# Seven products in place of eight: the experts' first matmuls by Strassen's scheme over 2x2 blocks, in three token passes

## The chip, the cores and the metric

The kernel runs on one core of a Trainium2 chip. The metric is the device time of one launch in microseconds (us). A core has five engines that run side by side and wait for each other by semaphores: TensorE (PE, with its weight loads shown apart as PEld), VectorE (DVE), ScalarE (ACT), GpSimd (POOL) and SyncE (SP), which here only issues the DMAs. Matmul results land in PSUM, eight banks of 512 float32 values per partition; DVE and ACT read them from there, POOL does not touch them in this kernel.

## The reference

Block-causal attention feeds a two-layer MLP with a leaky ReLU, and that feeds eight experts. Every token goes through every expert; a gate, normalised eight times over rows and columns (Sinkhorn), weighs the results.

```python
x = attention(q, k, v)                           # (2304, 512)
x = np.maximum(0.01 * h, h) @ w_out              # h = x @ w_in; (512, 2048), (2048, 512): the "GLU" stage here
logits = x @ w_gate                              # w_gate (512, 8)
P = np.exp(logits - logits.max())
for _ in range(8):
    P /= P.sum(1, keepdims=True) + 1e-09
    P /= P.sum(0, keepdims=True) + 1e-09
    P *= N / E
for e in range(8):                               # w1[e] (512, 1024), w2[e] (1024, 512)
    out += P[:, e:e + 1] * (np.maximum(x @ w1[e], 0.0) @ w2[e])
```

## The kernel before

The program has three stages. Attention comes first; it is the same in both kernels. Then comes the MLP, worked as two "experts" without a gate (e = 0 and 1, `NG` = 2), and then the eight real experts (e = 2 to 9). A float32 value is held as two float32r numbers, a high part and the rest, so a product of two values is three matmuls: high by high, high by low, low by high.

An expert is taken whole before the next. Its 2304 tokens go in five blocks (512, 512, 512, 384, 384), and the 1024 hidden columns in eight chunks of 128. `hidden(e, b, f)` (L483) multiplies one chunk of `w1` (stationary, four steps of 128 over the 512 inputs) with one block of tokens (moving): 4 x 3 = 12 matmuls into one bank of `ps_h`. ACT then takes the ReLU into the high part (L504), DVE the rest (L505). `second(e, b, f)` (L511) multiplies the hidden values (stationary, 128 tokens at a time) with 512 columns of `w2`: three matmuls for each 128 tokens (L525), summed over the eight chunks in up to four banks of `ps_o`. At the last chunk DVE multiplies each bank by its column of gate weights and adds it to the accumulator `acc` (L559). In the list `todo` the first products run two chunks ahead of the second ones.

The weights of the next expert are loaded during the last block (SP, 512 KB each), split by ACT (L118) and DVE (L119). The gate logits are float32r products of a split gate with the split tokens, 16 columns wide, turned back by float32 transposes (L566 to L586). The Sinkhorn steps follow one per chunk during the first expert; each column sum is one float32 matmul with a matrix of ones (L610).

The code gives a program order; a scheduler with a timeline model then sets the order of instructions on each engine, and each engine runs its own list strictly in order.

Of the kernel before, what the change touches and what calls it, by code (L numbers as in the profile page):

```python
# [15 lines left out]
P = 128  # L16
# [20 lines left out]
def block_attention_mlp_moe(  # L37
# [38 lines left out]
    xpool = ctx.enter_context(tc.tile_pool(name="xpool", bufs=1))  # L76
# [357 lines left out]
    n = 1  # L434
# [8 lines left out]
    with (  # L443
# [12 lines left out]
    hpool = ctx.enter_context(tc.tile_pool(name="hpool", bufs=4))  # L456
    gpool = ctx.enter_context(tc.tile_pool(name="gpool", bufs=1))
    ps_h = ctx.enter_context(tc.tile_pool(name="ps_h", bufs=4, space=bass.MemoryType.PSUM))
    ps_o = ctx.enter_context(tc.tile_pool(name="ps_o", bufs=1, space=bass.MemoryType.PSUM))

    acc = apool.tile([P, TT * DM], F32, name="acc")
    acc_x = acc.rearrange("p (c t) -> p c t", c=KC)
    acc_o = acc.rearrange("p (t d) -> p t d", d=DM)
    gate_raw = const.tile([P, KC, E], F32, name="gate_raw")
    gate = const.tile([P, KC, 2, E], F32R, name="gate")
# [6 lines left out]
    logl = const.tile([P, TT, E], F32, name="logl")  # L472

    nc.gpsimd.memset(ones, 1.0)
    nc.sync.dma_start(out=gate_raw, in_=w_gate.rearrange("(c p) e -> p c e", p=P))
    nc.gpsimd.tensor_copy(out=gate[:, :, 0, :], in_=gate_raw)
    nc.gpsimd.tensor_tensor(
        out=gate[:, :, 1, :], in0=gate_raw, in1=f32(gate[:, :, 0, :]), op=ALU.subtract
    )

    hid, o_ps = {}, {}

    def hidden(e, b, f):  # L483
# [13 lines left out]
        if e < NG:  # L497
            g = gpool.tile([P, 512], F32, name="g", tag="g")
            nc.scalar.activation(out=g[:, 0:n], in_=ps[:, 0:n], func=AF.Copy, scale=NEG_SLOPE)  # L499
            nc.vector.tensor_tensor(out=g[:, 0:n], in0=ps[:, 0:n], in1=g[:, 0:n], op=ALU.max)  # L500
            nc.scalar.copy(out=hi[:, 0:n], in_=g[:, 0:n])  # L501
            nc.vector.tensor_tensor(out=lo[:, 0:n], in0=g[:, 0:n], in1=f32(hi[:, 0:n]), op=ALU.subtract)
        else:
            nc.scalar.activation(out=hi[:, 0:n], in_=ps[:, 0:n], func=AF.Relu)  # L504
            nc.vector.scalar_tensor_tensor(  # L505
                out=lo[:, 0:n], in0=ps[:, 0:n], scalar=0.0, in1=f32(hi[:, 0:n]),
                op0=ALU.max, op1=ALU.subtract,
            )
        hid[e, b, f] = (hi, lo)

    def second(e, b, f):  # L511
        t0, n = blocks[b]
        wh, wl = (w.rearrange("p (j d) -> p j d", j=2)[:, f % 2, :] for w in w_part[2, e, f // 2])
        hi, lo = hid.pop((e, b, f))
        n_out = KC if e < NG else n // P
        for s in range(n_out):
            if f == 0:
                o_ps[s] = ps_o.tile([P, 512], F32, name=f"o{s}", tag=f"o{s}")
            cut = slice(s * P, (s + 1) * P)
            for m, (w, h) in enumerate(((wh, hi), (wl, hi), (wh, lo))):  # L520
                first, last = f == 0 and m == 0, f == FC - 1 and m == 2
                if e < NG:
                    nc.tensor.matmul(o_ps[s][:, 0:n], w[:, cut], h[:, 0:n], start=first, stop=last)  # L523
                else:
                    nc.tensor.matmul(o_ps[s], h[:, cut], w, start=first, stop=last)  # L525
            if f == FC - 1:
                evict(e, b, s)

    p_ready = [False]
    owed, later = [], []  # L530

    def evict(e, b, s):
        t0, n = blocks[b]
        if e < NG:
            a = acc_x[:, s, t0:t0 + n]
            if e == 0:
                nc.scalar.copy(out=a, in_=o_ps[s][:, 0:n])  # L537
                return
            nc.vector.tensor_tensor(out=a, in0=o_ps[s][:, 0:n], in1=a, op=ALU.add)
            if e < NG - 1:  # L540
                return

            def split():
                hi = xh[:, s, t0:t0 + n]
                nc.scalar.copy(out=hi, in_=a)
                nc.vector.tensor_tensor(out=xl[:, s, t0:t0 + n], in0=a, in1=f32(hi), op=ALU.subtract)

            later.append(split)
            return
        t = t0 // P + s  # L550
        x = e - NG
        a = acc_o[:, t, :]
        if x == 0 and not p_ready[0]:
            nc.scalar.copy(out=a, in_=o_ps[s])
            owed.append(t)
        elif x == 0:
            nc.vector.tensor_scalar(out=a, in0=o_ps[s], scalar1=pr[:, t, 0:1], scalar2=None, op0=ALU.mult)
        else:
            nc.vector.scalar_tensor_tensor(  # L559
                out=a, in0=o_ps[s], scalar=pr[:, t, x:x + 1], in1=a, op0=ALU.mult, op1=ALU.add  # L560
            )
        if x == E - 1:
            nc.sync.dma_start(out=out[t * P:(t + 1) * P, :], in_=a)


    def gate_block(b):  # L566
        t0, n = blocks[b]
        ps = ps_h.tile([P, 512], F32, name="l_ps", tag="h")
        for c in range(KC):
            for s, x in enumerate((xh, xl)):  # L570
                nc.tensor.matmul(  # L571
                    ps[0:2 * E, 0:n], gate[:, c].rearrange("p s e -> p (s e)"), x[:, c, t0:t0 + n],
                    start=c == 0 and s == 0, stop=c == KC - 1 and s == 1,
                )
        logT = gpool.tile([P, 512], F32, name="logT", tag="g")
        nc.scalar.copy(out=logT[0:2 * E, 0:n], in_=ps[0:2 * E, 0:n])
        m = n // P
        turned = ps_h.tile([P, 512], F32, name="t_ps", tag="h")
        for t in range(m):
            nc.tensor.transpose(  # L580
                turned[:, t * 2 * E:(t + 1) * 2 * E], logT[0:2 * E, t * P:(t + 1) * P], ident[0:2 * E, 0:2 * E]
            )
        both = turned[:, 0:m * 2 * E].rearrange("p (t s e) -> p t s e", s=2, e=E)
        ts = slice(t0 // P, t0 // P + m)
        nc.scalar.copy(out=logl[:, ts, :], in_=both[:, :, 1, :])
        nc.vector.tensor_tensor(out=pr[:, ts, :], in0=both[:, :, 0, :], in1=logl[:, ts, :], op=ALU.add)  # L586
# [8 lines left out]

    cs_ps = {}
# [11 lines left out]
    def sums():  # L608
        ps = ps_h.tile([P, 512], F32, name="c_ps", tag="h")
        nc.tensor.matmul(ps[:, 0:E], ones, st["cs"], start=True, stop=True)  # L610
        cs_ps[0] = ps

    def columns():
        cr = st["cr"]
        nc.vector.tensor_scalar(out=cr, in0=cs_ps[0][:, 0:E], scalar1=EPS, scalar2=None, op0=ALU.add)
        nc.vector.reciprocal(out=cr, in_=cr)
        nc.vector.tensor_tensor(
            out=pr, in0=pr, in1=cr.unsqueeze(1).to_broadcast([P, TT, E]), op=ALU.mult
        )
        nc.vector.tensor_scalar(out=pr, in0=pr, scalar1=float(NT) / E, scalar2=None, op0=ALU.mult)  # L620

    def settle():
        p_ready[0] = True
        for t in owed:
            a = acc_o[:, t, :]
# [3 lines left out]
    steps = [lambda: gate_block(NB - 1), gate_max, gate_exp]  # L629
    for _ in range(SINKHORN):  # L630
        steps += [rows, lambda: (sums(), columns())]
    steps.append(settle)


# [14 lines left out]
    for m, (e, b, f) in enumerate(todo):  # L649
# [20 lines left out]
        if later and f > 1:  # L670
            later.pop(0)()
# [35 lines left out]
```

## Time and profile before

| | us |
|---|---|
| three timed runs, median (lowest to highest) | 2255.51 (2254.02 to 2257.34) |
| the profiled execution | 2257.6 |
| its span, first to last instruction | 2255.8 |
| PE busy in the span | 2228.7 (99%) |
| PEld busy | 1898.6 (84%) |
| DVE busy | 803.9 (36%) |
| ACT busy | 549.1 (24%) |
| POOL busy | 135.1 (6%) |

The times are read against the span; the 1.8 us between span and time lie before the first and behind the last instruction. Matmuls are pipelined: one is drawn as 0.33 to 0.39 us long, but the next one starts before it ends, so the price of a matmul is the distance from its start to the start of the next. Attention and the change of float64 weights to float32 fill the first 250 us, the GLU stage goes on to about 670 us, and the experts take the rest.

### The profile page before, as it was taken

The numbers are of one execution on the slowest core, as the hardware profiler recorded it, in microseconds if no ns is written. First come the engines' busy times: TensorE is split into PE (matmuls) and PEld (weight loads), VectorE is DVE, ScalarE is ACT, GpSimd is POOL, SyncE is SP. The second block draws the span as 40 slices with busy tenths as digits, with TensorE's granted clock in tenths as the row PEclk, the third lists the DMA queues.
The fourth block names the chain that finished last, engine by engine and source line by source line (L and its number), as shares of the span: only waits on it lengthen the run. The fifth ranks groups of instructions, "written<-read, shape, count | busy, mean of one in ns | idle before, by whom it ended". The sixth has DMA issues, their size and how long they took to land.

```text
span 2255.8 us, 25881 instructions
## 1 busy us (share of the span) xinstructions
PE 2228.7 (99%) x10714; PEld 1898.6 (84%) x10714; DVE 803.9 (36%) x1514; ACT 549.1 (24%) x1145; POOL 135.1 (6%) x153
## 2 busy tenths in 40 slices
PE   7999999999999999999999999999999999999999
PEld 6777777988898898888888888888888888888888
DVE  8999666333351242123212312321231232123121
ACT  6777422332341112112111211211121121112110
POOL 3443321000000000000000000000000000000000
PEclk9999999999999999999999999999999999999999
DMA  4333143110020002002000200200020020001010
GB/s 106 87 87 73 52 125 119 38 38 1 1 75 1 1 10 66 1 1 66 10 1 10 66 1 1 66 10 1 10 66 1 1 66 10 1 10 47 19 38 28
DMA packets 106021, 79.28 MB, mean 35 GB/s; under 512 B 60592, under 2 KB 91312, under 8 KB 105904
## 3 DMA queue, kind: packets, MB, share of 16 engines
q1 hardware_dynamic: 105904, 77.63, 11.8%
q8 instruction: 84, 1.38, 0.3%
q14 instruction: 33, 0.27, 0.0%
HBM read 68.70 MB, written 8.91 MB: 34 GB/s over the span
## 4 chain that ended last, share of the span: by engine, by line
PE 84%; DVE 0%; ACT 0%; DVEq 0%; issue 0%
PE h_ps L491 42%; PE o L525 35%; PE o L523 7%; PE l_ps L571 0%; PE t_ps L580 0%; DVE acc L559 0%; PE c_ps L610 0%; DVEq L702 0%; ACT hh L501 0%; DVE g L500 0%; ACT acc L537 0%; DVE wb L153 0%
## 5 line engine op out<-in xcount | busy, mean ns | idle before, releaser
L491 PE MATMUL h_ps<-xh,w1h 128*128 128x512 f32 (+1 forms) x1600 | 590.9, 369 | 0.0
L491 PE MATMUL h_ps<-xh,w1l 128*128 128x512 f32 (+1 forms) x1600 | 589.5, 368 | 0.0
L491 PE MATMUL h_ps<-xl,w1h 128*128 128x512 f32 (+1 forms) x1600 | 589.1, 368 | 0.0
L505 DVE SCALAR_TENSOR_TENSOR hl<-h_ps,hh 128x512 fp32r<-128x512 f32 (+1 forms) x320 | 203.8, 637 | 948.0 <-ACT hh L504 947.9
L504 ACT ACTIVATE hh<-h_ps 128x512 fp32r<-128x512 f32 (+1 forms) x320 | 177.7, 555 | 1194.9 <-PE h_ps L491 1191.2
L525 PE MATMUL o<-w2l,hh 128*128 128x512 f32 x1152 | 450.4, 391 | 0.0
L525 PE MATMUL o<-w2h,hl 128*128 128x512 f32 x1152 | 449.3, 391 | 0.0
L525 PE MATMUL o<-w2h,hh 128*128 128x512 f32 x1152 | 446.9, 389 | 0.0
L491 PEld LDWEIGHTS h_ps<-xh,w1h 128*128 128x128 f32 x1600 | 301.1, 188 | 43.2
L491 PEld LDWEIGHTS h_ps<-xl,w1h 128*128 128x128 f32 x1600 | 300.8, 188 | 42.4
L491 PEld LDWEIGHTS h_ps<-xh,w1l 128*128 128x128 f32 x1600 | 300.7, 188 | 38.6
L525 PEld LDWEIGHTS o<-w2h,hl 128*128 128x128 f32 x1152 | 216.2, 188 | 45.3
L525 PEld LDWEIGHTS o<-w2l,hh 128*128 128x128 f32 x1152 | 216.3, 188 | 41.9
L525 PEld LDWEIGHTS o<-w2h,hh 128*128 128x128 f32 x1152 | 216.1, 188 | 41.2
L559 DVE SCALAR_TENSOR_TENSOR acc<-o,pr,acc 128x512 f32<-128x512 f32 x126 | 88.8, 744 | 119.4 <-PE o L525 119.4
L523 PE MATMUL o<-hh,w2h 128*128 128x512 f32 (+1 forms) x320 | 118.5, 370 | 4.6 <-ACT acc L537 4.6
L523 PE MATMUL o<-hh,w2l 128*128 128x512 f32 (+1 forms) x320 | 118.3, 370 | 0.0
L523 PE MATMUL o<-hl,w2h 128*128 128x512 f32 (+1 forms) x320 | 116.4, 370 | 0.0
L360 PE MATMUL av<-at,vz 128*128 128x448 f32 (+3 forms) x320 | 97.3, 428 | 0.0
L500 DVE TENSOR_TENSOR g<-h_ps,g 128x512 f32<-128x512 f32 (+1 forms) x80 | 50.8, 635 | 108.9 <-ACT g L499 108.7
L315 ACT ACTIVATE ex<-sc,nmax 128x288 f32<-128x288 f32 (+8 forms) x160 | 81.4, 515 | 29.7 <-DVE nmax L310 27.7
L499 ACT ACTIVATE g<-h_ps 128x512 f32<-128x512 f32 (+1 forms) x80 | 44.4, 555 | 143.1 <-PE h_ps L491 111.7
(110 smaller groups left out, 1643.3 us busy)
## 6 DMA issues: line engine op xcount, KB each, us to landing
wraw<-in_moe_w_dram SPq DMA_DIRECT2D x64, 512.0 KB, 3.6
wraw<-in_moe_w_in_dram SPq DMA_DIRECT2D x16, 512.0 KB, 3.9
wraw<-in_moe_w_out_dram SPq DMA_DIRECT2D x16, 512.0 KB, 3.7
out_dram<-acc SPq DMA_DIRECT2D x18, 256.0 KB, 2.1
qraw<-in_q_dram SPq DMA_DIRECT2D x32, 128.0 KB, 2.5
kraw<-in_k_dram SPq DMA_DIRECT2D x32, 128.0 KB, 2.5
vz<-in_v_dram SPq DMA_DIRECT2D x32, 128.0 KB, 2.4
s_in<-wa SPq DMA_DIRECT2D x8, 256.0 KB, 3.2
```

The costliest lines, as they stand in the source:

```text
L315: nc.scalar.activation(out=ex[p % 2][:, off[i] + lo:off[i] + hi], in_=part[s], func=AF.Exp, bias=nm[:, x:x + 1], scale=1.0, accum_out=sm[: ...
L360: nc.tensor.matmul(av[p][:, 512 + P * max(c - 1, 0):512 + S - P], lhsT, a[:, q0:, :], start=c == 0 and h == 0, stop=c == NKC - 1 and h == 1,)
L491: nc.tensor.matmul(ps[:, 0:n], w[:, c, cols], x, start=c == 0 and s == 0, stop=c == KC - 1 and s == 2,)
L499: nc.scalar.activation(out=g[:, 0:n], in_=ps[:, 0:n], func=AF.Copy, scale=NEG_SLOPE)
L500: nc.vector.tensor_tensor(out=g[:, 0:n], in0=ps[:, 0:n], in1=g[:, 0:n], op=ALU.max)
L504: nc.scalar.activation(out=hi[:, 0:n], in_=ps[:, 0:n], func=AF.Relu)
L505: nc.vector.scalar_tensor_tensor(out=lo[:, 0:n], in0=ps[:, 0:n], scalar=0.0, in1=f32(hi[:, 0:n]), op0=ALU.max, op1=ALU.subtract,)
L523: nc.tensor.matmul(o_ps[s][:, 0:n], w[:, cut], h[:, 0:n], start=first, stop=last)
L525: nc.tensor.matmul(o_ps[s], h[:, cut], w, start=first, stop=last)
L559: nc.vector.scalar_tensor_tensor(out=a, in0=o_ps[s], scalar=pr[:, t, x:x + 1], in1=a, op0=ALU.mult, op1=ALU.add)
```

## The change

The GLU stage stays as it was; its output now goes into three tiles `xa[0..2]` of 768 tokens (`TP`), each `[128, 4 x 768]` float32. Where a block of the GLU stage crosses a border between them, its eviction is cut in two.

The experts no longer run expert by expert over all tokens. Three passes of 768 tokens stand outside, the eight experts inside, and in each expert four groups of 256 hidden columns: 96 groups. In a group the first product is a 2x2 block product: `w1` is cut in 2 x 2 blocks (256 inputs by 128 hidden columns), the tokens in 2 x 2 blocks (256 inputs by 384 tokens). Strassen's scheme, in Winograd's form, needs seven block products for it, each two steps of 128 inputs by three matmuls, 384 columns wide, so 42 matmuls. They are named after the weight block that they use: A11, S1, A12, S2, S4, S3, A22. Three banks take them, and a bank is read while its sum is still growing: bank X takes A11 (ACT copies it out as `s1`), then S2 on top (copied as `s2`), then S3 (read for quarter 22), then A22 (quarter 21); bank Y takes S1 (copied as `s5`) and S4; bank Z takes A12. Three of the four quarters of the result add one kept copy on DVE before the ReLU (`c11`, `c12`, `c22`).

The sums of weight blocks are made by POOL, four subtractions or additions of 256 columns for each group, and then split by ACT and DVE. The sums of token blocks are made once per pass (`x_step`): four subtractions of 768 columns on POOL, seven splits of 768 columns on ACT and DVE, into the place where the split input of the GLU stage stood (`xpart` in place of `xpool`). The splits of the next pass are made in the last group of the pass before.

The second products stay 512 wide with three matmuls for each 128 tokens and 128 hidden columns. They are now `combine(n, t)`: twelve matmuls for one tile of 128 tokens, over the two groups of a pair, three tiles in each group and two to three groups behind the first products. Each tile is then added to the output once per pair of groups.

The weights of an expert are loaded and split once per pass, so three times. The gate is a native float32 product: the tokens are stationary, the eight gate columns moving, 72 matmuls of 8 columns (`gate_part`), with no transposes.

```diff
-    todo = [(e, b, f) for e in range(NE) for b in range(NB) for f in range(FC)]
+    todo = [(e, b, f) for e in range(NG) for b in range(NB) for f in range(FC)]
...
+    def gate_part(p, t0, n, ps):
+        for t in range(t0, t0 + n):
+            for c in range(KC):
+                nc.tensor.matmul(
+                    ps[:, t * E:(t + 1) * E], xv[p][:, c, t * P:(t + 1) * P], gate[:, c, :],
+                    start=c == 0, stop=c == KC - 1,
+                )
...
+    groups = [(p, e, i) for p in range(NPASS) for e in range(E) for i in range(NI)]
+    terms = ("A11", "S1", "A12", "S2", "S4", "S3", "A22")
...
+            nc.gpsimd.tensor_tensor(out=one[:, 0], in0=a21, in1=a22, op=ALU.add)
+            nc.gpsimd.tensor_tensor(out=one[:, 1], in0=one[:, 0], in1=a11, op=ALU.subtract)
+            nc.gpsimd.tensor_tensor(out=two[:, 0], in0=a11, in1=a21, op=ALU.subtract)
+            nc.gpsimd.tensor_tensor(out=two[:, 1], in0=a12, in1=one[:, 1], op=ALU.subtract)
...
+        return [
+            sums,
+            part("A", 0, 2, lambda: t["raw"][:, :, 0:P]),
+            part("A", 2, 3, lambda: t["raw"][:, 2:4, P:2 * P]),
+            part("S", 0, 2, lambda: t["one"]),
+            part("S", 2, 4, lambda: t["two"]),
+        ]
...
+        if change:
+            nc.gpsimd.tensor_tensor(out=src, in0=change[0], in1=change[1], op=ALU.subtract)
+        hi, lo = (xpart.tile([P, 2, HT], F32R, name=f"x{n}{k}", tag=f"x{n}{k}") for n in "hl")
+        nc.scalar.copy(out=hi, in_=src)
+        nc.vector.tensor_tensor(out=lo, in0=src, in1=f32(hi), op=ALU.subtract)
...
+    def product(n, k, name, first):
+        if first:
+            bank[n, name] = ps_h.tile([P, 512], F32, name="h_ps", tag="h")
+        ps = bank[n, name][:, 0:HT]
+        (wh, wl), (bh, bl) = wq.pop((n, k)), bq[groups[n][0], k]
+        for c in range(2):
+            for s, (w, x) in enumerate(((wh, bh), (wh, bl), (wl, bh))):
+                nc.tensor.matmul(
+                    ps, w[:, c], x[:, c], start=first and c == 0 and s == 0, stop=c == 1 and s == 2,
+                    skip_group_check=True,
+                )
+    def keep(n, name, k):
+        t = part[n, k] = mpool.tile([P, HT], F32, name=k, tag=k)
+        nc.scalar.copy(out=t, in_=bank[n, name][:, 0:HT])
+    def quarter(n, k, name, add):
+        x = bank[n, name][:, 0:HT]
+        if add:
+            c = mpool.tile([P, HT], F32, name=f"c{k}", tag=f"c{k}")
+            nc.vector.tensor_tensor(out=c, in0=x, in1=part[n, add], op=ALU.add)
+            x = c
...
+        nc.scalar.activation(out=hi, in_=x, func=AF.Relu)
+        nc.vector.scalar_tensor_tensor(out=lo, in0=x, scalar=0.0, in1=f32(hi), op0=ALU.max, op1=ALU.subtract)
...
+        product(n, "A11", "X", True)
+        keep(n, "X", "s1")
...
+        units[0]()
+        if n:
+            tail(n - 1)
...
+        units[1]()
...
+        product(n, "S1", "Y", True)
+        keep(n, "Y", "s5")
+        product(n, "S2", "X", False)
+        keep(n, "X", "s2")
...
+        units[2]()
...
+        product(n, "A12", "Z", True)
+        quarter(n, "11", "Z", "s1")
+        product(n, "S4", "Y", False)
+        quarter(n, "12", "Y", "s2")
+        product(n, "S3", "X", False)
+        quarter(n, "22", "X", "s5")
```

How the change moves the order on the engines, at three places. A number behind a name only tells one buffer of that name from another.

First, PE in the middle of the experts. Before, twelve first products (`h_ps`, 384 or 512 wide) and the second products of one chunk (`o0` to `o3`) take turns; these rows are such a border:

```order
L491 MATMUL h_ps_11727<-xh_70,w1h_10863 128x384
L491 MATMUL h_ps_11727<-xl_71,w1h_10863 128x384
L491 MATMUL h_ps_11727<-xh_70,w1l_10864 128x384
L525 MATMUL o0_11537<-w2h_11069,hh_11682 128x512
L525 MATMUL o0_11537<-w2l_11070,hh_11682 128x512
L525 MATMUL o0_11537<-w2h_11069,hl_11683 128x512
```

In the changed kernel this is the start of an even group of pass 1. Behind S3 of the group before (here left out) and A11 stand two half-done tiles, `o1` and `o2`, which read the older group (`h12_11743`, `h22_11754`); these rows are their end and what follows:

```order
L708 MATMUL o2_11942<-w2l_11630,h22_11754 128x512
L708 MATMUL o2_11942<-w2h_11629,h22_11754 128x512
L672 MATMUL h_ps_11958<-xhS1_10427,w1h_11801 128x384
L672 MATMUL h_ps_11958<-xlS1_10428,w1h_11801 128x384
L672 MATMUL h_ps_11958<-xhS1_10427,w1l_11802 128x384
L672 MATMUL h_ps_11958<-xhS1_10427,w1h_11801 128x384
L708 MATMUL o1_11909<-w2h_11766,h12_11880 128x512
L708 MATMUL o1_11909<-w2l_11767,h12_11880 128x512
L708 MATMUL o2_11942<-w2h_11766,h12_11880 128x512
L672 MATMUL h_ps_11757<-xhA22_10553,w1h_11666 128x384
L672 MATMUL h_ps_11757<-xlA22_10554,w1h_11666 128x384
L708 MATMUL o1_11909<-w2h_11766,h12_11880 128x512
```

The quarters of the group just finished (`h12_11880`, and later `h22_11891`) are read only after A11, twelve second products and most of S1, and A22 of the group before is pushed in between.

Second, DVE at the same place. Before, there is one instruction per chunk (`hl`) and now and then an eviction into `acc`:

```order
L505 SCALAR_TENSOR_TENSOR hl_10276<-h_ps_10262,hh_10275 128x512
L559 SCALAR_TENSOR_TENSOR acc_2962<-o0_10101,pr_2965,acc_2962 128x512
L505 SCALAR_TENSOR_TENSOR hl_10305<-h_ps_10291,hh_10304 128x512
L559 SCALAR_TENSOR_TENSOR acc_2962<-o1_10105,pr_2965,acc_2962 128x512
L559 SCALAR_TENSOR_TENSOR acc_2962<-o2_10109,pr_2965,acc_2962 128x512
L559 SCALAR_TENSOR_TENSOR acc_2962<-o3_10113,pr_2965,acc_2962 128x512
```

After, the three additions and the lower parts of the quarters stand among the splits of the weights of later groups:

```order
L685 TENSOR_TENSOR c11_11867<-h_ps_11860,s1_11764 128x384
L685 TENSOR_TENSOR c12_11878<-h_ps_11821,s2_11836 128x384
L691 SCALAR_TENSOR_TENSOR h11_11869<-c11_11867,h11_11869 128x384
L685 TENSOR_TENSOR c22_11889<-h_ps_11757,s5_11828 128x384
L691 SCALAR_TENSOR_TENSOR h12_11880<-c12_11878,h12_11880 128x384
L640 TENSOR_TENSOR w1l_11941<-wraw_11858,w1h_11940 128x512
L640 TENSOR_TENSOR w1l_11941<-wraw_11858,w1h_11940 128x256
L119 TENSOR_TENSOR w2l_12041<-wraw_11907,w2h_12040 128x1024
L691 SCALAR_TENSOR_TENSOR h22_11891<-c22_11889,h22_11891 128x384
```

Three weight splits have come between `h12` and `h22`, both of which the second products above read.

Third, DVE where the GLU stage ends. Before, the evictions of the last block (`acc<-o`) and the split of its four parts (`xl`) stand among the first experts' work:

```order
L505 SCALAR_TENSOR_TENSOR hl_6042<-h_ps_6028,hh_6041 128x512
L539 TENSOR_TENSOR acc_2962<-o0_5818,acc_2962 128x384
L505 SCALAR_TENSOR_TENSOR hl_6079<-h_ps_6065,hh_6078 128x512
L539 TENSOR_TENSOR acc_2962<-o1_5822,acc_2962 128x384
L539 TENSOR_TENSOR acc_2962<-o2_5826,acc_2962 128x384
L546 TENSOR_TENSOR xl_71<-acc_2962,xh_70 128x384
```

After, the token blocks of pass 0 (`xl` and a term's name) are split there, 768 columns at a time, and the last GLU chunk's `hl` stands among them:

```order
L500 TENSOR_TENSOR g_5979<-h_ps_5964,g_5979 128x384
L660 TENSOR_TENSOR xlA11_6040<-xa0_2962,xhA11_6039 128x768
L660 TENSOR_TENSOR xlA12_6049<-xa0_2962,xhA12_6048 128x768
L660 TENSOR_TENSOR xlS4_6058<-xa0_2962,xhS4_6057 128x768
L119 TENSOR_TENSOR w2l_6303<-wraw_6196,w2h_6302 128x1024
L502 TENSOR_TENSOR hl_5978<-g_5979,hh_5977 128x384
L660 TENSOR_TENSOR xlS1_6045<-xa0_2962,xhS1_6044 128x768
L660 TENSOR_TENSOR xlS3_6063<-xa0_2962,xhS3_6062 128x768
L525 TENSOR_TENSOR xa2_2964<-o0_5796,xa2_2964 128x384
L525 TENSOR_TENSOR xa2_2964<-o1_5800,xa2_2964 128x384
```

Seven splits of 768 columns have moved into a stretch that had splits of 384.

## Rows read from the trace of the kernel before

**Rows 1.** Busy time in the experts' stretch: engine busy (instructions), clock, DMA share, GB/s.
```profile
700.00:2230.00 1530.00, 1530.00 (x7075) 1307.30 (x7074) 371.70 (x581) 235.74 (x380) 0.38 (x1) 1.00 0.07 22
```

**Rows 2.** Longest wait of the run: engine line <- releaser: us, times, longest.
```profile
ACT hh L504 <- PE h_ps L491: 1191.2, 291, 5.1
```

**Rows 3.** Timeline of PE, 512 wide, 48 matmuls apart: start, length, instruction.
```profile
960.63 0.39 PE L491 MATMUL h_ps<-xh,w1h 128*128 128x512 f32 x1
...
971.51 0.39 PE L491 MATMUL h_ps<-xh,w1h 128*128 128x512 f32 x1
```

**Rows 4.** Timeline of PE, 384 wide, 37 matmuls apart.
```profile
443.79 0.33 PE L491 MATMUL h_ps<-xh,w1h 128*128 128x384 f32 x1
...
450.20 0.33 PE L523 MATMUL o<-hh,w2l 128*128 128x384 f32 x1
```

**Rows 5.** Busy time over one whole expert, columns as in rows 1.
```profile
960.79:1158.32 197.53, 197.53 (x913) 168.83 (x913) 46.73 (x68) 30.23 (x48) 0.00 (x0) 1.00 0.07 22
```

**Rows 6.** Timeline of PE around a float32 matmul, 8 columns wide.
```profile
733.75 0.39 PE L525 MATMUL o<-w2h,hl 128*128 128x512 f32 x1
...
733.97 0.28 PE L610 MATMUL c_ps<-cs,ones 128*128 128x8 f32 x2
...
734.43 0.39 PE L491 MATMUL h_ps<-xl,w1h 128*128 128x512 f32 x1
```

**Rows 7.** Timeline of PE around the gate's transposes.
```profile
705.58 0.39 PE L525 MATMUL o<-w2h,hh 128*128 128x512 f32 x1
...
705.90 0.35 PE L580 MATMUL t_ps<-ident,logT 16*128 16x16 f32 x3
...
706.52 0.39 PE L491 MATMUL h_ps<-xl,w1h 128*128 128x512 f32 x1
```

**Rows 8.** Groups by shape, experts: count | busy us, mean ns | idle before.
```profile
L559 DVE SCALAR_TENSOR_TENSOR acc<-o,pr,acc 128x512 f32<-128x512 f32 x123 | 86.8, 744 | 114.7 <-PE o L525 114.7
L505 DVE SCALAR_TENSOR_TENSOR hl<-h_ps,hh 128x384 fp32r<-128x384 f32 x124 | 68.9, 556 | 258.1 <-ACT hh L504 258.0
L504 ACT ACTIVATE hh<-h_ps 128x384 fp32r<-128x384 f32 x124 | 60.8, 491 | 325.2 <-PE h_ps L491 321.5 <-DVE hl L505 3.7
L119 DVE TENSOR_TENSOR w1l<-wraw,w1h 128x1024 fp32r<-128x1024 f32 x28 | 34.3, 1223 | 78.8 <-ACT w1h L118 78.8
L602 DVE RECIPROCAL rs<-rs 128x18 f32<-128x18 f32 x8 | 2.1, 267 | 0.3
```

**Rows 9.** Groups by shape, GLU stage from 440 us on, columns as in rows 8.
```profile
L546 DVE TENSOR_TENSOR xl<-acc,xh 128x512 fp32r<-128x512 f32 x12 | 7.8, 685 | 0.1
L545 ACT CAST xh<-acc 128x512 fp32r<-128x512 f32 x12 | 7.4, 622 | 3.3 <-DVE acc L539 3.2
```

**Rows 10.** Timeline of POOL and DVE in the GLU stage.
```profile
258.05 0.26 POOL L477 TENSOR_TENSOR gate<-gate_raw,gate 128x32 fp32r<-128x32 f32 x1
...
260.94 1.30 POOL L190 TENSOR_TENSOR wa<-wa,w2h 128x512 f32<-128x512 f32 x1 [2.64 <-ACT g L499]
261.46 1.33 DVE L171 SCALAR_TENSOR_TENSOR wb<-wraw,wb 128x512 f32<-128x512 uint32 x1
...
334.95 0.68 DVE L171 SCALAR_TENSOR_TENSOR wb<-wraw,wb 128x512 f32<-128x512 uint32 x1
```

**Rows 11.** DMA issues: out<-in, count, size, median us to landing.
```profile
wraw<-in_moe_w_dram SPq DMA_DIRECT2D x64, 512.0 KB, 3.6
```

**Rows 12.** Busy time (DVE, ACT) of instructions on the gate tile in the Sinkhorn stretch.
```profile
706.60:827.50 120.90, 13.05 (x42) 0.42 (x1) 1.00 0.00 1
```

**Rows 13.** Line 590 on POOL: duration ns min/median/max, first and last start.
```profile
L590 POOLq MODIFY_POOL_CONFIG  x2: 11/11/11, 383.7 to 383.8; - x2
L590 POOL PARTITION_ALL_REDUCE gall<-gmax x1: 382/382/382, 707.2 to 707.2; - x1
```

**Rows 14.** Timeline of the end of the run.
```profile
2250.16 0.84 PE L525 MATMUL o<-w2h,hl 128*128 128x512 f32 x3
2250.59 2.07 DVE L559 SCALAR_TENSOR_TENSOR acc<-o,pr,acc 128x512 f32<-128x512 f32 x3 [4.63 <-PE o L525]
```

More of the change, by code (lines that the diff above doesn't have):

```diff
@@ L520, in second @@
             for m, (w, h) in enumerate(((wh, hi), (wl, hi), (wh, lo))):
[L521 to L525, printed above, removed]
-            if f == FC - 1:
[L527 to L563, printed above, removed]
@@ L566, in gate_block @@
-    def gate_block(b):
-        t0, n = blocks[b]
-        ps = ps_h.tile([P, 512], F32, name="l_ps", tag="h")
[L569 to L586, printed above, removed]
+                nc.tensor.matmul(
+                    o_ps[s][:, 0:n], w[:, cut], h[:, 0:n], start=f == 0 and m == 0, stop=f == FC - 1 and m == 2
+                )
@@ L622, in settle @@
     def settle():
-        p_ready[0] = True
         for t in owed:
-            a = acc_o[:, t, :]
+            a = xo[0][:, t, :]
             nc.vector.tensor_scalar(out=a, in0=a, scalar1=pr[:, t, 0:1], scalar2=None, op0=ALU.mult)
         owed.clear()
[L629 to L632, printed above, removed]
-    NE = NG + E
     late = [(2, f) for f in range(2, FC)]
@@ L659, in block_attention_mlp_moe @@
                 split_later.append((which, e + 1, f // 2))
+        if last and e + 1 == NG:
+            if f == 1:
+                w1_load(0)
+                w2_load(0)
+            if f == 3:
+                for s in w1_steps(0):
+                    s()
+                w1_load(1)
         if e == 0 and b == 0:
@@ L669, in block_attention_mlp_moe @@
                     bits.pop(0)()
[L670 to L676 removed]
+        if e == NG - 1 and f == FC - 1 and b in (2, 3):
+            gate_pass(b - 2)
+    assert not bits
+    gpool.release()
+    hpool.release()
+    xpool.release()
+    xpart = tc.alloc_tile_pool(name="xpart", bufs=1, side="right", reuse_waits="tile")
@@ new lines, in block_attention_mlp_moe, with gate_last @@
+    hpool1 = tc.alloc_tile_pool(name="hpool1", bufs=3, side="right", reuse_waits="tile")
+    mpool = tc.alloc_tile_pool(name="mpool", bufs=1, reuse_waits="tile")
+    hpool2 = tc.alloc_tile_pool(name="hpool2", bufs=3, reuse_waits="tile")
+    norm = [gate_max, gate_exp]
+    for _ in range(SINKHORN):
+        norm += [rows, columns]
+    g_ps = {}
+    def gate_last(t0):
+        if t0 == 0:
+            g_ps[0] = o_bank()
+        gate_part(2, t0, 2, g_ps[0])
+        if t0 + 2 == TC:
+            gate_take(2, g_ps[0])
@@ L680 @@
+    tail(NGR - 1)
+    for t in [*range(TC // 2, TC), *range(TC // 2)]:
+        combine(NGR - 2, t)
+    assert not norm and not owed
+    for pool in (hpool2, mpool, hpool1, xpart):
+        pool.release()
 _INS = ["q", "k", "v", "moe_w_in", "moe_w_out", "moe2_w_gate", "moe2_w1", "moe2_w2"]
```

218 lines of the change are left out of this document (177 added, 41 removed).

## The prediction

> **What bounds the kernel now.** I read the busy times by stretch first: in 1530 us of the experts' stretch PE is busy for 1530.00, its granted clock is 1.00 (the 2.4 GHz level), while DVE is busy for 372, ACT for 236 and POOL for nothing [rows 1]. The list of waits says the same from the other side: the longest wait of the run is ACT waiting for PE [rows 2]. So the experts are a queue on PE, and only what PE has to issue counts until some other engine becomes late. A busy PE is no measure of its speed, so I took prices from the timeline, start to start. 48 matmuls of 512 columns lie 971.51 - 960.63 = 10.88 us apart, 0.2267 each [rows 3]; 37 of 384 columns lie 6.41 us apart, 0.1732 each [rows 4]. The difference, 0.0535 us for 128 columns, is 2.4 columns per ns; what is left over is 0.013 us per matmul, the price of more and narrower matmuls. One expert takes 197.53 us [rows 5]; its 720 wide and 192 narrow matmuls make 163.2 + 33.3 = 196.5 by these prices, so they carry all but 1.0 us.
>
> **First products.** Before, each of 8 experts has 8 chunks x 12 matmuls x 5 blocks: 2304 of 512 and 1536 of 384 columns, 522.2 + 266.1 = 788.3 us. After, 96 groups x 7 products x 6 matmuls = 4032 of 384 columns, 698.5 us. That is 89.8 less. If the 1.0 us per expert belongs to the wide matmuls, their price is 0.2282 and the gain 93.3; I take 90. The second products keep their number, 3456, and their width.
>
> **Gate.** It removes 24 matmuls of 512 and 16 of 384 columns (8.2 us) and five sets of transposes. One set costs the distance 705.58 to 706.52 less two wide matmuls, 0.94 - 0.45 = 0.49 [rows 7], 2.4 in all. It adds 72 float32 matmuls of 8 columns. The trace has eight of the kind, drawn as two each; one costs 734.43 - 733.75 = 0.68, less two wide matmuls, 0.23 [rows 6]. Back to back they could be a little cheaper or dearer; 72 x 0.23 = 16.6. Net +6.0 (bounds +3 and +9). All of it is on PE.
>
> **What the other engines get.** Per group PE has 42 narrow and 36 wide matmuls: 7.3 + 8.2 = 15.4 us. DVE has, per group: `w1` splits of three times 512 and once 256 columns, 3 x 0.685 + 0.42 (the step from 1.223 at 1024 to 0.685 at 512 carried down) = 2.5; the `w2` split 1.22; three additions and four lower parts of 384 columns, 7 x 0.556 = 3.9; three evictions at 0.744 = 2.2 [rows 8, 9]. Sum 9.8 of 15.4. ACT, at 0.622 and 0.491 for its pieces [rows 8, 9] and 1.1 for a split of 1024 (0.622 in DVE's proportion), has about 6.8. POOL's four sums of 256 columns cost about 0.75 each, between 0.26 for 32 and 1.30 for 512 columns [rows 10]: 3.0. The three-fold weight traffic is two 512 KB loads per group; one lands in 3.6 us [rows 11], so 7.2 of 15.4, on an SP queue that otherwise holds only the 18 output DMAs. None of these exceeds PE, so in the steady groups I cost them at nothing; their cover is PE's 15.4 us. What would be late next is DVE: behind S4 the chain to the last-needed value, the lower part of `h22`, is two additions, two lower parts, two `w1` splits, one `w2` split and itself, 5.1 us and its handovers, and the order gives PE S3, A11 and some 7 us of second products, S1 and A22, 9 us in all, before it is read. That leaves 3 us of slack.
>
> **The border to the experts, and the Sinkhorn steps.** From the last GLU first product to the end of group 5 PE has 36 narrow second products (6.2), groups 0 and 1 without second products but with 24 gate matmuls (7.3 + 5.5 + 7.3), four full groups (61.8) and eight column sums (1.8): 90 us. DVE has seven token splits of 768 columns at 0.95 (6.7), six groups of splits and quarters (6 x 7.6 = 45.7), six evictions (4.1), the GLU's rest (2.8), the final scaling of six tiles (4.1) and the Sinkhorn steps: 13.1 us on the gate tile [rows 12] and 32 short ones at some 0.2 [rows 8]. Together 83 of 90. Group 1 is the tight one: DVE 7.6 + 3.2 against PE's 7.3, so DVE falls 3.5 us behind there, and PE's in-order queue holds a column sum that needs DVE's result. I take 4 us of PE waits, between 0 (the splits start under the GLU's last 6.2 us) and 12 (POOL's sums in the way as well, below).
>
> **Pass borders.** In the last group of a pass DVE has 9.8 + 6.7 = 16.5 against 15.4; twice 1.1 at most, 0 at least, since only the next group's use decides. I take 1.
>
> **The end.** Now the last three matmuls feed three evictions that queue on DVE, 2250.59 + 2.07, some 1.7 us behind PE's end at 2251.0 [rows 14]. After, twelve matmuls lie between evictions and only one of 0.74 is left: -0.9.
>
> **Sum.** -90 + 6 + 4 + 1 - 0.9 = -79.9. The profiled execution took 2257.6, which gives 2177.7; it lies 2.1 above the median of the runs, so against the median 2175.6. I say 2176.
>
> **Two rules of the skill.** Between 260.94 and 262.24 POOL adds two SBUF tiles; a DVE instruction with two SBUF operands that begins at 261.46 takes 1.33 us, and the same with POOL idle 0.68 [rows 10]. The Trainium skill (SBUF — State Buffer, section "SBUF: two separate sides") says that GpSimd and such a DVE instruction take one pair of ports as a lock, and the loser waits for the whole instruction; the trace agrees, with 0.65 us lost. It is the first rival below.
> POOL's all-reduce of the gate took 0.38 us, but its configuration had been changed 323 us earlier [rows 13]; the changed order has that change right before it and one back right after. The Trainium skill (GPSIMD Engine Reference, section "2.1 Instruction dispatch") says the first call after such a change pays about 6 us that no row shows. No row here tests it. By it the sum would be up to 6 us higher, 2182, an estimate from that page, inside the forecast's own range; I give it 1 in 4 of the forecast's chance. The change back would be hidden, as group 3's sums are needed a group later.
>
> **Rivals.**
> *POOL locks out DVE in the steady groups* (chance 0.18). For it: the 1.33 us row; each group has 3.0 us of POOL beside 5.4 us of DVE work on two SBUF operands (w1, w2, and the lower parts that read `c`). Against: even 9.8 + 3.0 = 12.8 stays under 15.4, and the slack at `h22` is 3 us. If one POOL sum of 0.75 falls into the chain in each of the 48 even groups where it is read soonest, 36 us: 2212.
> *The cross-engine chain on DVE becomes the bound* (0.06, the slower side). Of DVE's 15 instructions per group, 12 read what ACT has written, and the queue is strict: if each idles DVE for one ACT instruction of 0.49, that is 5.9 us, and 9.8 + 3.0 + 5.9 = 18.7 per group against 15.4, 3.3 x 96 = +317: 2493. It decides from 12.8 + 2.6 on, and the kernel is slower than before from 12.8 + 3.5, since 80 us are to be eaten by 96 groups. For it: before, DVE waited for ACT for 258 us in rows of this shape alone [rows 8]; against: those were waits for PE's pace, and the order puts weight splits between the steps of the chain.
> *The products don't get cheaper with fewer columns* (0.03, slower too): if something other than columns set the pace, for example a matmul that adds to a bank just read, 4032 x 0.2267 = 914 instead of 698.5: 2391. Against it stand 0.1732 at 384 columns, and the copies of a bank lie under at least one other product.
>
> **How the numbers follow.** The forecast gets 0.73, and from its bounds (gain 93.3 and no waits, to waits of 12 and 4) 2165 to 2192. The lock's middle and most of its range lie above; I draw the range from 2164 to 2208, which leaves out most of the slow cases (0.09) and the upper half of the lock. About 0.2%, 4.5 us, is what a measurement can tell from no change; the first two cases lie far below 2251, so faster gets 0.90, with 0.01 kept back; of the two slow cases 0.08 end slower and 0.01 near no change, so within 0.2% gets 0.02.
>
> **What will show it.** Right: PE busy near the whole experts' stretch, narrow first products 0.173 apart, a full group in 15.4 to 15.6 us, an expert of a pass in 62; DVE near two thirds, POOL near a fifth. The waits that PE has lie in the first 40 us of the experts. The lock would show as DVE instructions of twice their length beside POOL's sums and PE idle before a second product that reads `h12` or `h22`, 48 times. Wrong altogether would be a group of more than 16 us, or first products more than 0.19 apart.

## The result, and the profile after

The changed kernel takes 2214.64 us (median of 4 runs, 2211.59 to 2216.18) against 2255.18 before: a ratio of 0.9817 [0.98, 0.9834], 40.5 us less. The forecast was 2176 with a range from 2164 to 2208: the direction held, about half of the gain did not come.

The profiled execution took 2214.53 us. Busy time of each engine over the span (share, instructions), and the same over the passes through the experts, with columns as in [rows 1]:

```profile
PE 2185.7 (99%) x10992; PEld 1932.6 (87%) x10992; DVE 1320.0 (60%) x2429; ACT 899.5 (41%) x1902; POOL 471.9 (21%) x547
```
```profile
700.00:2150.00 1450.00, 1450.00 (x7172) 1301.99 (x7171) 864.32 (x1462) 584.07 (x1127) 311.93 (x376) 1.00 0.23 70
```

PE is busy for all of 1450 us at the full clock, and the list of its waits in that stretch is empty. DVE has 60%, POOL 21%, DMA traffic went from 22 to 70 GB/s. So no other engine became the bound, and yet the time is missing. The chain of work that ended last shows where (start, length, what): the same run of 24 narrow products returns once per group.

```profile
1003.31 4.24 PE h_ps L672 x24
...
1019.13 4.24 PE h_ps L672 x24
...
1034.90 4.24 PE h_ps L672 x24
```

Two groups take 1034.90 - 1003.31 = 31.59 us, 15.795 each, where the forecast had 15.44. The 24 narrow products take 0.1767 each and not the 0.1732 of [rows 4]. PE's time from the first GLU product to the last matmul, each matmul counted from its start to the next start, by kind (us; a wait is what a start lies behind its usual place):

| | before | after | aligned | aligned, gate spread |
|---|---|---|---|---|
| GLU products | 399.5 | 405.4 | 399.3 | 396.6 |
| gate | 10.0 | 20.6 | 20.6 | 15.0 |
| first products | 792.9 | 716.7 | 710.0 | 707.6 |
| second products | 788.5 | 804.3 | 795.2 | 795.0 |
| column sums | 1.1 | 1.1 | 1.1 | 1.1 |
| waits | 5.1 | 5.6 | 6.2 | 7.6 |
| sum | 1997.0 | 1953.7 | 1932.4 | 1923.0 |

(The last two columns are experiments below.) First products lost 76.2 us and not 90. The second products, same number and same width, cost 15.8 us more, and so did the GLU, whose code did not change, with 5.9. The gate cost 10.6 and not 6; waits cost 0.5 and not 5.

The gate shows in the granted clock. Windows of the border (columns as above), and the timeline of PE (start, length, instruction):

```profile
595.00:600.00 5.00, 5.00 (x36) 4.68 (x35) 3.04 (x6) 0.51 (x1) 0.00 (x0) 0.92 0.00 0
600.00:605.00 5.00, 5.00 (x24) 5.00 (x24) 0.21 (x1) 0.00 (x0) 0.00 (x0) 0.50 0.00 0
605.00:610.00 5.00, 5.00 (x19) 5.00 (x18) 0.56 (x1) 0.78 (x2) 0.00 (x0) 0.55 0.00 0
```
```profile
596.64 7.88 PE L539 MATMUL l_ps<-gate,xa 128*128 128x8 f32 x48
604.37 0.67 PE L492 MATMUL h_ps<-xh,w1h 128*128 128x384 f32 x1
604.84 0.52 PE L492 MATMUL h_ps<-xl,w1h 128*128 128x384 f32 x1
605.16 0.52 PE L492 MATMUL h_ps<-xh,w1l 128*128 128x384 f32 x1
```

In the first burst of 24 gate matmuls (drawn as 48) the clock falls to half (the 1.2 GHz level), and the GLU products behind it lie 0.32 apart instead of 0.173. Between 595 and 700 us the clock was at half in four stretches: 10.2, 6.8, 3.4 and 6.8 us. Three begin in a burst of the gate or between its last pieces, the one at 681.1 follows PE's only wait at the border, 2.0 us for the first token split of S1:

```profile
PE h_ps L672 <- ACT xhS L659: 2.0, 1, 2.0
```

The first rival, POOL locking out DVE, is not there in the steady groups. Groups by shape, columns as in [rows 8]:

```profile
L691 DVE SCALAR_TENSOR_TENSOR h<-c,h 128x384 fp32r<-128x384 f32 x277 | 152.7, 551 | 0.0
L640 DVE TENSOR_TENSOR w1l<-wa,w1h 128x512 fp32r<-128x512 f32 x184 | 120.4, 695 | 204.2 <-ACT w1h L639 204.2
...
L617 POOL TENSOR_TENSOR wa<-wraw 128x256 f32<-128x256 f32 x92 | 97.6, 1060 | 1099.0 <-DVE w1l L640 1089.2 <-DMA wraw<-in_moe_w_dram 9.8
```

DVE's pieces take 0.551 and 0.695, as in [rows 8, 9] (0.556, 0.685). It is POOL that gets longer: the first of its four sums takes 1.06, the others some 0.75 as forecast, and in these groups PE waits for none. At the border, where splits of 768 and 1024 columns stand beside POOL's sums, both engines get longer (start, length):

```profile
678.37 2.83 DVE L119 TENSOR_TENSOR w2l<-wraw,w2h 128x1024 fp32r<-128x1024 f32 x1
```
```profile
676.17 1.45 POOL L618 TENSOR_TENSOR wa<-wa,wraw 128x256 f32<-128x256 f32 x1
677.60 2.52 POOL L657 TENSOR_TENSOR xa<-xa 128x768 f32<-128x768 f32 x1
```

In the mean of the passes the split of 1024 columns takes 1.26, POOL's sum of 256 columns 0.74, and a sum of 768 columns 1.84. At the pass borders it is DVE that loses: a split of 1024 columns beside such a sum takes 2.43, and PE waits for none of it. The chain of the 2.0 us wait goes through these two POOL instructions to ACT's split and PE. So the rival's mechanism is in the trace; by these lengths its price for PE is some 1.4 of those 2.0 us, an estimate.

### The profile page after: what moved, and what is told of

Its sections match the earlier page's. It is cut to its first block, busy times and chain, and to the rows that moved or that the text cites. A ratio compares the mean times of both kernels' runs of the same rounds, so it can differ in the third digit from the quotient of the medians.

```text
span 2212.7 us, 29298 instructions
## 1 busy us (share of the span) xinstructions
PE 2185.7 (99%) x10992; PEld 1932.6 (87%) x10992; DVE 1320.0 (60%) x2429; ACT 899.5 (41%) x1902; POOL 471.9 (21%) x547
## 4 chain that ended last, share of the span: by engine, by line
PE 83%; POOL 0%; ACT 0%; DVE 0%; issue 0%; POOLq 0%; ACTq 0%
PE o L708 36%; PE h_ps L672 32%; PE h_ps L492 7%; PE o L514 7%; PE l_ps L539 1%; PE o L539 0%; POOL xa L657 0%; POOL wa L618 0%; POOL wa L617 0%; PE o L574 0%; POOL wa L619 0%; ACT xhS L659 0%; DVE xa L721 0%; DVE w1l L640 0%; ACT w1h L639 0%
## 5 line engine op out<-in xcount | busy, mean ns | idle before, releaser
L708 PE MATMUL o<-w2h,h 128*128 128x512 f32 x2304 | 767.6, 394 | 0.0
L708 PEld LDWEIGHTS o<-w2h,h 128*128 128x128 f32 x2304 | 431.6, 188 | 82.0
L708 PE MATMUL o<-w2l,h 128*128 128x512 f32 x1152 | 455.4, 396 | 0.0
L672 PE MATMUL h_ps<-xhS,w1h 128*128 128x384 f32 x768 | 261.4, 341 | 2.0 <-ACT xhS L659 2.0
L672 PE MATMUL h_ps<-xhS,w1l 128*128 128x384 f32 x768 | 261.4, 340 | 0.0
L672 PE MATMUL h_ps<-xlS,w1h 128*128 128x384 f32 x768 | 261.2, 340 | 0.0
L708 PEld LDWEIGHTS o<-w2l,h 128*128 128x128 f32 x1152 | 216.2, 188 | 38.0
L672 PE MATMUL h_ps<-xhA,w1h 128*128 128x384 f32 x576 | 195.5, 339 | 0.0
L672 PE MATMUL h_ps<-xlA,w1h 128*128 128x384 f32 x576 | 195.5, 339 | 0.0
L672 PE MATMUL h_ps<-xhA,w1l 128*128 128x384 f32 x576 | 195.5, 339 | 0.0
```

The source lines that it names most:

```text
L672: nc.tensor.matmul(ps, w[:, c], x[:, c], start=first and c == 0 and s == 0, stop=c == 1 and s == 2, skip_group_check=True,)
L708: nc.tensor.matmul(o, h, w, start=m == 0, stop=m == 11)
```

## Experiments

All ratios are to the kernel before, run on the same chip.

**1. Start addresses.** In the built program the token parts `xh`, `xl`, later `xhA11` and the like, and the quarters `h11`, `h12`, `h21` start 32 bytes past a multiple of 64; they lie on SBUF's right side, whose top is at 229344. `w1` starts at multiples of 128, `w2` at odd or even multiples of 64; in the kernel before everything starts at a multiple of 128. The GLU is the hint: same code, same instructions, but its wide first products went from 0.2267 to 0.233 apart (twelve of them from 2.72 to 2.80 us).

```diff
+    rpad = ctx.enter_context(tc.tile_pool(name="rpad", bufs=1, side="right"))
+    rpad.tile([P, 8], F32, name="rpad")      # align64; align128: 24, and 16 on the left
     xpool = tc.alloc_tile_pool(name="xpool", bufs=1, side="right")
```

> The changed kernel with 32 unused bytes at the top of the right side of SBUF, so that the token parts and three of the four hidden quarters start at multiples of 64 bytes, where in the changed kernel they start 32 bytes past one. Nothing else differs. Theory A (start addresses: an operand that starts 32 bytes past a multiple of 64 makes each matmul 3 to 6 ns dearer): products of 384 columns fall from 0.1767 us apart to 0.173, of 512 from 0.2330 to 0.227, GLU included; 96 groups x (42 x 3.4 + 36 x 6.3 ns) = 35 us and some 6 us in the GLU: about 2174. Theory B (SBUF traffic of the other engines and of three times the weight transfers slows the reads): nothing changes, 2214. Theory C (it is the alternation of 384 and 512 columns, as in the kernel before's last two blocks, 0.1756 and 0.2310): only the part above those is gained, about 17 us: 2197.

> The changed kernel with 96 unused bytes at the top of the right side of SBUF and 64 on the left, so that every operand of the products starts at a multiple of 128 bytes, as in the kernel before. Theory A: as with multiples of 64 if 64 is what counts (about 2174), some microseconds less than that if 128 counts. Theory B: 2214. Theory C: 2197 for both.

Measured: 2198.41 us (0.9749 [0.9735, 0.9764]) and 2196.43 (0.974 [0.9726, 0.9755]); 16 and 18 us less for bytes that nobody reads. Theory B falls. The groups take 15.65 and 15.63: there C's figure is the one that came. But the two kernels reach it by different ways. One run of 24 narrow and the 17 wide products behind it, in the chain of the changed kernel, of `align64` and of `align128`:

```profile
1003.31 4.24 PE h_ps L672 x24
1007.55 3.96 PE o L708 x17
```
```profile
1000.61 4.16 PE h_ps L674 x24
1004.77 3.96 PE o L710 x17
```
```profile
1027.65 4.18 PE h_ps L675 x24
1031.83 3.90 PE o L711 x17
```

With multiples of 64 the narrow products get all of their settled price back and the wide ones of the groups next to nothing: they stay at some 0.232, though no two operands differ modulo 64 any more. Twelve wide first products of the GLU take 2.75. Only with multiples of 128 do the wide products settle at 0.2267, in the GLU (2.72) and in the groups. So theory A is right for narrow products at 64, and for wide ones only at 128. The same narrow run, in the changed kernel and in the one aligned to 128 (called the aligned kernel from here on), every sixth matmul of PE's timeline:

```profile
1018.97 0.34 PE L672 MATMUL h_ps<-xhA,w1h 128*128 128x384 f32 x1
...
1020.03 0.34 PE L672 MATMUL h_ps<-xhS,w1h 128*128 128x384 f32 x1
...
1021.09 0.34 PE L672 MATMUL h_ps<-xhS,w1h 128*128 128x384 f32 x1
...
1022.15 0.34 PE L672 MATMUL h_ps<-xhA,w1h 128*128 128x384 f32 x1
```
```profile
1011.83 0.33 PE L675 MATMUL h_ps<-xhA,w1h 128*128 128x384 f32 x1
...
1012.90 0.33 PE L675 MATMUL h_ps<-xhS,w1h 128*128 128x384 f32 x1
...
1013.94 0.33 PE L675 MATMUL h_ps<-xhS,w1h 128*128 128x384 f32 x1
...
1014.98 0.33 PE L675 MATMUL h_ps<-xhA,w1h 128*128 128x384 f32 x1
```

In the changed kernel six take 1.06 throughout and never settle. Aligned, the first six behind a wide run take 1.07 and then 1.04, which is 0.1733 each. In the aligned kernel, then, what is left above the settled prices stands behind the changes of width and passes. The two are not independent: in `align64` the first six narrow products behind a wide run take 1.042 (median), 2 ns above the settled price.

**2. Is it the address, or the distance between two?**

```diff
+    const.tile([P, 8], F32, name="pad")       # before32: moves everything by 32 bytes
+    xpool.tile([P, 8], F32, name="pad0")      # before_x32: moves xh and xl alone
     xh = xpool.tile([P, KC, NT], F32R, name="xh")
     xl = xpool.tile([P, KC, NT], F32R, name="xl")
+    xpool.tile([P, 24], F32, name="pad1")     # before_x32
```

> The kernel before with 32 unused bytes ahead of all its SBUF tiles, so that every operand starts 32 bytes past a multiple of 64. Nothing else differs. Theory A: its wide matmuls rise from 0.2267 to about 0.232, its narrow ones from 0.1745 to 0.177; 6912 x 5.5 + 2304 x 2.5 ns = 44 us, about 2299. Theories B and C: no change, 2255.

> The kernel before with 32 unused bytes ahead of the token parts xh and xl and 96 behind them: they alone start 32 bytes past a multiple of 64, their weights at a multiple of 64 as before. Moving every operand by 32 bytes changed nothing (2254.0 against 2255.2). Theory A2 (what counts is that the operand that streams and the one that is loaded as weights lie 32 bytes apart modulo 64): 2880 wide first products rise from 0.2267 to 0.2327, 1920 narrow ones by 2 to 3.4 ns, and three second products after each run by 6 ns: 17.3 + 5 + 4 = 26 us, 2281. If the shifted kernel's 0.2267 showed that starts don't count at all and the gain of the aligned kernels came from some other displacement: 2255.

Measured: 2253.98 (0.9997 [0.9988, 1.0007]), theory A as put is wrong; and 2275.42 (1.0096 [1.0081, 1.0111]), 21.8 us more, where A2 said 26. The chain of the kernel with `xh` and `xl` alone moved, in a wide stretch:

```profile
906.32 2.81 PE h_ps L493 x12
909.13 2.73 PE o L527 x12
911.86 2.81 PE h_ps L493 x12
```

First products, whose two operands lie 32 bytes apart modulo 64, take 0.234; second products, whose operands are aligned, 0.2275, close to the settled 0.2267. So between these two kernels it is the distance that counts, for wide products. It is not the whole rule: in `align64` no distance modulo 64 is left, and the groups' wide products do not settle. The 5 us that A2 had for narrow ones didn't come: they settle at 0.1733 in this kernel, and the first six behind a wide run take 1.043 where the kernel before takes 1.066, so all narrow first products together get 2.6 us cheaper. Why narrow ones suffer in the changed kernel and not here is open.

**3. The gate's price.** Three kernels leave the gate's 72 matmuls out.

```diff
-            gate_pass(b - 2)
+    nc.vector.memset(pr, 0.0)                 # nogate, nogate_align
+    nc.vector.tensor_scalar(out=..., in0=xa[2][:, 0:TT * E], scalar1=0.0, ...)   # nogate_late
```

> The changed kernel without the gate's 72 float32 matmuls and their five evictions; the gate tile is set to zero instead, and the Sinkhorn steps run on that. Theory D (the gate's narrow matmuls pull the granted clock to half for 27 us of the stretch from 599 to 698 us): the half-clock stretches at 599, 643 and 691 go, and the time falls by 16 us for the matmuls and some 12 for the clock: about 2187. If the clock there falls for another reason, only the matmuls go: 2199.

> The aligned kernel (2196.4) without the gate's 72 matmuls and their evictions; the gate tile is set to zero at the border instead, and the Sinkhorn steps run on that. In the earlier run without the gate the zeroing stood in DVE's queue ahead of the GLU and cost PE a wait of 7.6 us and half-clock stretches behind it, which this one leaves out. Theory D: 72 x 0.218 = 15.7 us and about 12 of the clock go: 2168. If only the matmuls count: 2181.

> The aligned kernel with the spread gate (2183.2), now without the gate's 72 matmuls and evictions; the gate tile is set to zero from the last GLU output, so that the zeroing can't stand ahead of the GLU as in the two earlier runs without the gate. PE spends 15.05 us on the gate's matmuls in the spread kernel's trace: 2168. If they cover PE's waits for the first token splits: between 2170 and 2176, with those waits grown.

Measured: 2202.24 us, 2184.69 and 2167.56 (0.9613 [0.9597, 0.9629]). The first two don't give the price: a gate tile of zeros waits for nothing, so the scheduler put the zeroing and the first Sinkhorn steps ahead of the GLU (in the second run too, though written later). One of these steps is POOL's all-reduce, whose configuration is changed at 254.5 us. POOL then idles twice without a wait that the profile shows (first run):

```profile
260.57 0.38 POOL L557 PARTITION_ALL_REDUCE gall<-gmax  x1 [6.03 <-issue]
268.72 1.25 POOL L190 TENSOR_TENSOR wa<-wa,w2h 128x512 f32<-128x512 f32 x1 [7.78 <-issue]
```

DVE waited for it, and PE 7.6 us for DVE, with half-clock stretches behind. The idle times stand right behind the two changes of configuration (254.5 and 260.9 us), so by this trace these cost the wait, and not the zeroing itself. On the clock the first run does answer: at its border 3.4 us at half are left, behind four waits of 4.5 us in all; the stretches that began in the gate's bursts are gone. The third, against the spread gate, gives 15.6 us beside the 15.05 of the table's last column: 0.209 per matmul.

**4. The clock.** One tile of 128 tokens at a time instead of bursts:

```diff
-        if e == NG - 1 and f == FC - 1 and b in (2, 3):
-            gate_pass(b - 2)
+        if e == NG - 1 and f >= 2 and b in (2, 3):
+            gate_tile(b - 2, f - 2)
...
+        if n == 0:
+            gate_last(3)                      # likewise behind the other products of group 0
```

> The kernel with every operand at a multiple of 128 bytes (2196.4), and the gate's 72 float32 matmuls no longer in bursts of 24, 24 and three times 8, but four at a time (one tile of 128 tokens) behind a GLU chunk or a first product. Theory D (bursts of narrow matmuls pull the clock down, 27 us at half of it between 595 and 695 us in the aligned kernel's profile): the half-clock stretches go but for one after a wait, 2184. Rival (the matmuls are slow wherever they stand, and the clock falls around each): 2196 or more.

Measured: 2183.15 us (0.9688 [0.9674, 0.9703]), 13.3 less than aligned alone. Windows of its border:

```profile
560.00:600.00 40.00, 40.00 (x212) 35.18 (x211) 11.54 (x23) 7.69 (x14) 0.00 (x0) 1.00 0.00 1
600.00:640.00 40.00, 40.00 (x250) 40.00 (x249) 13.10 (x29) 9.06 (x19) 0.00 (x0) 1.00 0.04 14
...
670.00:680.00 10.00, 9.23 (x57) 8.90 (x57) 6.88 (x10) 3.93 (x8) 4.45 (x2) 0.83 0.01 2
```

The clock stays at 1.00 through 48 of the gate's matmuls; 3.4 us at half remain behind the waits at 664 to 672 and behind some of the last 24 gate matmuls, which stand closer together there; the run without gate matmuls (`nogate_late`) has 3.4 us too, behind its waits. The table's columns account for 9.4 of the 13.3 us; in the aligned kernel's profiled run the GLU also began 2.9 us later, after a half-clock stretch of the attention, whose code is the same.

**5. The change of width.** The second products of a group in one run of 36 instead of three of 12:

```diff
-        units[0]()                            # behind A11; units[1] behind A22, units[2] behind S2
+        product(n, "S1", "Y", True)
+        tail(n - 1)
+        units[0](); units[1](); units[2]()    # with the weight steps between them
+        product(n, "S2", "X", False)
```

> The aligned kernel with the spread gate, and in each group the three second-product runs of 12 matmuls put into one run of 36, with A11, S1 and A22 ahead of it and S2, A12, S4 and S3 behind it; four long-lived PSUM banks take the place of the rotating ones. Theory C (each change of width costs: in the aligned kernel's profile the first nine matmuls of 512 after narrow ones take 40 ns more than nine settled ones, the first six narrow ones 27 ns more): four of six changes per group go, 96 x 2 x 0.067 = 12.9 us less than with the spread gate alone, about 2171. If the extra does not come from the change of width: as with the spread gate alone, 2184. If DVE's work, now bunched, comes late: PE waits in each group, and 2190 or more.

Measured: 2187.09. The edit did not do what it says: the scheduler interleaved the products again, with 8.0 changes of width per group (8.9 before it). The next kernels hold PE to the written order by an edge from each block's matmuls to the last of the block ahead.

> The kernel with one run of 36 second products per group, and now with edges that hold PE to the order in which the groups are written. Without them the scheduler had interleaved the products again: about 8 changes of width per group in the aligned kernel and in the first version of this one, against 2 here. Theory C2 (after a change of width the first nine matmuls of 512 columns take 40 ns more in all and the first six of 384 take 27 ns more, the rest is settled at 0.2267 and 0.1733): 0.19 us above settled per group becomes 0.067, 96 x 0.125 = 12 us less than with the spread gate alone (2183.2): 2171, if PE waits for nobody; each 0.1 us of wait per group takes 10 us back.

> The aligned kernel with the spread gate, PE held to the order in which the changed kernel's groups are written: three runs of 12 second products per group, 6 changes of width instead of some 9. Theory C2: all six runs of each group are long enough for the whole extra (3 x 40 + 3 x 27 = 201 ns), so there is no gain over 2183.2 although a third of the changes is gone. Rival (each change costs alike): 192 ns x 1/3 x 96 = 6 us less, 2177.

> The kernel with one run of 36 second products per group, PE held to that order from group 6 on only; the border and the Sinkhorn steps are left to the scheduler. Held from group 1 on, the steady groups had no waits and 2 changes of width each, but the border had 7.5 us more of PE waits and 19 us more at half clock, and the whole took 2188.9. Theory C2: the waits and the half clock of the border go and the settled groups stay: about 2173, 10 us under the 2183.2 of the spread gate alone. If the held order itself costs in the steady groups: 2183 or more.

Measured: 2188.87, 2262.41 and 2186.20 us (0.969 [0.9672, 0.9708]). In the groups theory C2 is right. The chain of the third:

```profile
1001.53 7.30 PE h_ps L691 x42
1008.84 8.20 PE o L733 x36
1017.04 7.30 PE h_ps L691 x42
1024.34 8.20 PE o L733 x36
```

A group takes 15.507 us, 15.44 and the 0.067 of two changes. But the gain of 0.124 a group, 12 us, is spent elsewhere: held to the order, PE waits at each border of a pass,

```profile
PE o L733 <- DVE h L713: 4.1, 2, 2.1
PE h_ps L691 <- DVE c L707: 1.6, 3, 0.7
```

and each of the two long waits brings 3.4 us at half clock; the border to the experts had 13.7 us at half clock against 3.4. With six held runs PE waits all along,

```profile
PE o L732 <- ACT h L711: 20.2, 43, 1.1
PE o L732 <- DVE h L712: 18.4, 45, 4.5
```

and the kernel is slower than before (1.0036 [1.0022, 1.0049]), so its time says nothing on the price of a change. Its trace does: the first six narrow products of a run take 1.066 (median), the first nine wide ones 2.081, as in the kernel with two changes. Changes do not all cost alike: with 8.9 of them the extra is 0.19 a group, 0.021 each, with two long runs 0.033 each. And the run says something else: the scheduler's interleaving, not the order that the groups are written in, is what covers the chain over the weight loads, ACT and DVE; of the chain from 720 to 2200 us weight loads and splits of `w2` are 25%, in the kernel of experiment 4 nothing.

It is the width that counts, and not the turn from first to second products: in the kernel before, where both are 512 wide, they take turns every twelve matmuls, and no extra shows (its chain):

```profile
906.39 2.72 PE h_ps L491 x12
909.11 2.72 PE o L525 x12
```

The best of these kernels is the one of experiment 4, 2183.15 us.

## Why the prediction was wrong

The step that failed is the price in "Per group PE has 42 narrow and 36 wide matmuls: 7.3 + 8.2 = 15.4 us". The two prices came from stretches in which every product has one width and every operand is aligned [rows 3, 4]; a group of the changed kernel has neither. It took 15.795. Of the 0.355 us missing per group, 34 us in all, alignment to 128 bytes takes back 0.165 (16 us, experiment 1), and the 0.19 left (18 us) stands behind the changes of width (experiment 5). The addresses also cost the GLU 6 us. For the token parts they come from the one line of the change that seemed to do nothing, their move to the right side; the quarters and `w2` are new tiles, off multiples of 128 too.

- *First products, -90.* The count was right, and the settled price of a narrow product too: 0.1733. -76.2 came. The sentence "The second products keep their number, 3456, and their width" was true and the conclusion from it false: +15.8.
- *The 1.0 us per expert that the two prices left over* was the sign. The kernel before changes width 34 times per expert, in its last two blocks; behind such a change nine wide matmuls take 40 ns more in all and six narrow ones 27: 34 x 0.033 = 1.1 us. I moved it to the wide products' price or let it stand, and did not ask what it was.
- *Gate, +6.* The 16.6 for 72 matmuls was good (15.05 at full clock). That bursts of them take the clock down was not thought of: 13.3 us between the medians of burst and spread, 9.4 of them in the table.
- *Border, +4, and passes, +1.* 2.0 us of wait, and none at the passes. The 6 us that the prediction held possible for the all-reduce cost nothing: its configuration is changed at 689.3 us, and POOL waits 5.70 us for DVE's maximum anyway. Where nothing else holds POOL up, in `nogate`, they are there, 6.03.
- *End, -0.9.* From the start of the last matmul to the end of the profiled span 4.3 us, before 5.2.
- *The other engines at nothing.* Right in the groups; DVE is at 60% of the passes. Their traffic does not slow PE there: at 70 GB/s of DMA against 22, the aligned kernel's settled products lie 0.1733 and 0.2267 apart, as before. The Trainium skill (SBUF — State Buffer, section "Who interferes with whom") says that PE waits for nobody at SBUF; as to other engines these distances agree, but PE's own two operands are another matter.
- *Rivals.* The lock is not in the steady groups; it is at the border, where it is part of the 2.0 us. The chain over DVE is no bound in the scheduler's order and is part of one, with the weight loads, in the order with six held runs. Narrow products did get cheaper.

By the table against the forecast's terms: first products 13.8 short, second 15.8, GLU 5.9, gate 4.6, waits 4.5 better: 35.6 of the 36.8 us by which the profiled execution missed the sum of 2177.7.

What stays open: what in the chip makes the operands' addresses, or a change of width, cost these nanoseconds, and by which rule of addresses; and how the clock's part divides between matmuls at half clock and the shift of the run's beginning.

## What to carry to other kernels

Take a matmul's price from a stretch with the mixture of widths that the new kernel will have, and follow up each remainder per unit until it has a name. When a change moves a pool, compare the start addresses of the operands of the inner loop modulo 128 before and after. Short float32 matmuls go one small piece at a time between long ones, not in bursts.

## What the runs showed of the hardware that was not expected

- Wide float32r products lie 0.2267 us apart with every operand at a multiple of 128 bytes, or all 32 bytes past one (2253.98 against 2255.16 us). With the moving operand alone 32 bytes off they lie 0.234 apart (2275.42). In `align64`, with every operand at a multiple of 64, some not at one of 128, the groups' wide ones stay at some 0.232, and the narrow ones settle at 0.1733.
- After a change from 384 to 512 columns or back, nine (six) matmuls take 40 (27) ns more in all, with operands aligned to 128 bytes and without a wait; then the old distance is back. With the token parts alone moved by 32 bytes, or in `align64`, the six narrow ones take only 2 to 3 ns more.
- The granted clock fell to half (the 1.2 GHz level) in both bursts of 24 float32 matmuls of 8 columns, with PE busy all the while; with the same 48 matmuls four at a time between GLU products it stayed at 1.00.
